# A long convolution ahead of two MLPs: first-stage chunks of four channels with one copying engine each, single-stepped weight conversion, deeper buffers for x, filter copies on ScalarE

## The chip, the cores and the metric

The kernel runs on one core of one Trainium2 chip. The core has a matrix engine (TensorE, in profiles PE, its weight loads PEld), VectorE (DVE), ScalarE (ACT), GpSimd (POOL) and SyncE (SP, which here only issues DMAs), and 16 DMA engines behind the queues. Matmul results land in PSUM, which TensorE writes, and which VectorE and ScalarE read; everything else lies in SBUF. The metric is the device time of one execution in microseconds.

## The reference

```python
# _attn_ref, S = 12480, D = 128, filter order 64
h_mlp = np.maximum(pos_emb @ w1, 0.0) @ w2
h_filt = h_mlp * np.exp(-0.01 * pos)[:, None]
u = x * v
Uf = np.fft.rfft(u, n=2 * S, axis=1)
Hf = np.fft.rfft(h_filt, n=2 * S, axis=0)
y = np.fft.irfft(Uf * Hf[None], n=2 * S, axis=1)[:, :S]
x = x * y                                   # 12480 x 128
# _moe_ref, d_ff = 2048: a rational function between two products
h = x @ w_in
g = (a0 + a1*h + a2*h**2 + a3*h**3) / (1 + |b0|*|h| + |b1|*h**2 + 1e-6)
x = g @ w_out
# _moe2_ref: leaky ReLU between two products
h = x @ w_in2
out = np.maximum(0.01 * h, h) @ w_out2
```

The four weight matrices come as float64; the kernel turns them to float32 with integer operations on their two 32-bit halves.

## The kernel before

The convolution is a transform of length N1 x N2 = 179 x 128, done in two stages, for two groups of 64 channels (`g` = 0 and 1) one after the other. Work runs through one instruction stream per engine in the order of the program, so an instruction also waits for everything that stands ahead of it on its engine.

Filter MLP (to about 29 us): `pos` is loaded by SP in pieces, VectorE multiplies it with the window (line 449), TensorE transposes and multiplies, ScalarE copies and applies the ReLU into `rh`. VectorE clears `hf[64:]` at line 441. At line 422 to 458 GpSimd does small memsets.

Inputs: `load_u(c)` and `make_u(c)`, lines 460 to 473, handle chunk `c` of 16. `XV` has three buffers, each for x and v of two mirrored halves of four positions. SP loads x (four DMAs) and v (four DMAs), GpSimd multiplies them (line 468), VectorE adds and subtracts the halves into `u` (line 471, writing one word every 128), and then `load_u(c + 3)` is issued.

Filter stage (29 to 96 us, lines 529 to 545): eleven rounds, each of up to six positions. TensorE multiplies `rh` with `w2b` into a PSUM tile `hps`; VectorE copies the first channel group into `hf` (line 537), ScalarE copies the second one (line 542) and issues its store to DRAM, `hsc`; then comes one `make_u`, whose loads are queued on SP.

Four passes of `first(g, s, c, cn)` (lines 601 to 610): pass (0,1) for the filter of group 0, pass (0,0) for u of group 0, then, after the spectrum stage, pass (1,0) and pass (1,1). Each goes through 64 channels in chunks of six, 11 or 12 of them. For each channel there are two matmul instructions into a PSUM tile `ap` (two buffers of three banks); ScalarE copies partitions 0 to 63 with both parts at once (line 608), VectorE copies partitions 64 to 127 in two instructions (609, 610). In pass (1,0) GpSimd copies the second filter half from where it was reloaded (`raw`, from `hsc`) into `hf`, four instructions at line 753.

Spectrum stage `second_stage(g)`: 23 steps. Step b multiplies four frequencies (`xp`), ScalarE copies the filter half (643), VectorE makes two products (650), GpSimd adds and subtracts (656 to 658), and the inverse of step b-3 follows: TensorE into the single PSUM buffer `gp`, ScalarE copies a part (671), VectorE adds (673) into one of two `gs` buffers, and SP stores it to `bd`. SP also loads the tables `c_m` three steps ahead.

Weight conversion: 16 pieces. `conv_w(c)` issues six VectorE instructions (580 to 590) and two on GpSimd (594, 597); `conv(2)` first queues the store of the piece before on SP, then converts, then queues the load of the piece two ahead, into the buffer just read. Whole pieces are called at certain chunks of the passes and after steps 4, 8, 12, 16 and 20 of spectrum stage 0.

After `second_stage(1)` (to about 430 us) comes the main stage, the two MLPs, in an order planned by `plan()`.

The tile framework lets two engines that touch the same PSUM bank of one tile go one after the other, in program order.

Of the kernel before, what the change touches and what calls it, by code (L numbers as in the profile page):

```python
# [20 lines left out]
D = 128  # L21
# [276 lines left out]
def conv_moe_moe(ctx: ExitStack, tc: tile.TileContext, I, out, dbg=None):  # L298
# [52 lines left out]
    with tc.manual_schedule():  # L351
# [89 lines left out]
        dve.memset(hf[64:], 0.0)  # L441

        dve.tensor_scalar(out=w2b[:64, 1], in0=w2b[:64, 1], scalar1=-1.0, scalar2=None, op0=ALU.mult)
# [31 lines left out]
        for c in range(3):  # L475
            load_u(c)
# [45 lines left out]
        uc = 3  # L522
# [6 lines left out]
        for c in range(0, 64, 6):  # L529
            cn = min(6, 64 - c)  # L530
            hps = ps_b.tile([128, 6, 2, NG, DG], F32, tag="b", name=f"hps{c}")
            for i in range(cn):
# [8 lines left out]
            hs = cut(Aw, 128 * c, [cn, 2, DG])[:NH]  # L541
            act.copy(hs, hps[:NH, :cn, :, 1])
            spread(act, hsc[:, c : c + cn], hs)
            make_u(uc)
            uc += 1
# [8 lines left out]
        raws, wst = {}, []  # L554
# [17 lines left out]
        def conv_w(c):  # L572
            if c >= 4 * NQ:
                return
# [5 lines left out]
            dve.tensor_scalar(out=ex, in0=hi, scalar1=0x7FF00000, scalar2=None, op0=ALU.bitwise_and)  # L580
            dve.tensor_scalar(out=sc, in0=hi, scalar1=-0x80000000, scalar2=None, op0=ALU.bitwise_and)

            dve.tensor_scalar(
                out=hm, in0=hi, scalar1=0xFFFFF, scalar2=0x100000, op0=ALU.bitwise_and, op1=ALU.bitwise_or
            )
            dve.tensor_scalar(out=ex, in0=ex, scalar1=float(896 << 20), scalar2=0.0, op0=ALU.subtract, op1=ALU.max)
            dve.scalar_tensor_tensor(
                out=w0, in0=lo.bitcast(U32), scalar=2.0**-32, in1=hm, op0=ALU.mult, op1=ALU.add
            )
            dve.scalar_tensor_tensor(  # L590
# [7 lines left out]
            wst.append((wsc[k, :, q * QW : (q + 1) * QW], w))  # L598


        def first(g, s, c, cn):
            ap_ = ps_b.tile([128, 6, 256], F32, tag="b", name=f"ap{g}_{s}_{c}")
            for i in range(cn):
                lhs = hf[:, c + i] if s else u[:NU, g * DG + c + i]
                pe.matmul(ap_[:, i, : 2 * K1], lhs, f1t if s else f1, start=True, stop=True)
            a = ap_[:, :cn, : 2 * K1].rearrange("p d (r k) -> p r k d", r=2)
            dst = Ak[:, 1 - s, :, :, c : c + cn]
# [4 lines left out]
        def chunks(end):  # L612
            c = 0
            for cn in [6] * 9 + end:
                yield c, cn
                c += cn
# [464 lines left out]
```

## Time and profile before

| | |
|---|---|
| median of three runs | 1779.72 us (1779.49 to 1779.74) |
| the profiled execution | 1783.21 us, its span 1781.4 us |
| busy over the span: PE, DVE, ACT, POOL | 1637.5, 1509.6, 1400.9, 1408.2 us |
| mean granted clock of TensorE | 0.96 |
| bytes moved by DMA | 97.12 MB, mean 55 GB/s |

The span counts from the first to the last instruction of the core. [...] In a stretch table, "busy" of one engine can be compared with the length of the stretch; a stretch in which no engine is near full is one in which they wait for each other or for DMAs. In a timeline, the text in brackets is the idle time of the engine before the instruction, and what ended it.

### The profile page before, as it was taken

Reading aid. Unit: us, or ns where it says so; the run is one execution under the profiler, and the core shown is the slowest. Engines: PE = TensorE matmul, PEld = TensorE weight load, DVE = VectorE, ACT = ScalarE, POOL = GpSimd, SP = SyncE. Lnnn points to the kernel's source line nnn. Section 1 sums busy time; section 2 is a strip of 40 time slices with the busy share of each in tenths; the row PEclk is TensorE's granted clock in tenths of the full one; section 3 lists DMA queues with packets and bytes.
Section 4 is the critical chain, followed back from the end, with each engine's and each line's share of the span. In section 5 each row is a group of like instructions: output and inputs, shape, how many; then the busy total and the mean of one; then the engine's idle time right before and its main releaser. Section 6 shows DMA issues by size and latency. Waiting matters only on the chain.

```text
span 1781.4 us, 21425 instructions
## 1 busy us (share of the span) xinstructions
PE 1637.5 (92%) x6394; PEld 1144.6 (64%) x6394; DVE 1509.6 (85%) x2481; ACT 1400.9 (79%) x2556; POOL 1408.2 (79%) x1205
## 2 busy tenths in 40 slices
PE   6666777698799999999999999999999999999999
PEld 4356656576556666666666666666666666666666
DVE  6456656765799999999999999999999999999993
ACT  3145215533799999999999999999999999999995
POOL 2422555265799999999999999999998999999993
PEclk9777989898799999999999999999999999999999
DMA  6532461266111111101111111011111110110000
GB/s 174 176 114 89 149 189 63 95 221 186 37 25 29 29 29 25 27 12 29 29 29 34 29 25 27 7 34 29 29 29 34 25 29 6 29 29 6 5 5 14
DMA packets 89599, 97.12 MB, mean 55 GB/s; under 512 B 53200, under 2 KB 58326, under 8 KB 88642
## 3 DMA queue, kind: packets, MB, share of 16 engines
q1 hardware_dynamic: 87462, 92.65, 19.0%
q10 hardware_dynamic: 2020, 3.09, 0.5%
q8 instruction: 51, 0.84, 0.2%
q14 instruction: 66, 0.54, 0.1%
HBM read 70.65 MB, written 25.07 MB: 54 GB/s over the span
## 4 chain that ended last, share of the span: by engine, by line
PE 71%; DVE 2%; ACT 1%; POOL 1%; issue 0%; DMA 0%; SPq 0%; ACTq 0%; DVEq 0%; POOLq 0%
PE o1p L951 18%; PE o2p L951 14%; PE h L480 10%; PE h L482 10%; PE h L481 10%; PE yP L906 3%; PE o2p L482 1%; PE o2p L481 1%; PE o2p L480 1%; PE oP L1028 1%; PE xP L899 1%; DVE g L1002 1%; DVE v L989 1%; DVE wk L984 0%; POOL wk L987 0%
## 5 line engine op out<-in xcount | busy, mean ns | idle before, releaser
L987 POOL TENSOR_TENSOR wk<-wk 128x980 f32<-128x980 f32 (+1 forms) x208 | 471.7, 2268 | 55.7 <-DVE wk L984 54.0
L951 PE MATMUL o1p<-g,wo 128*128 128x490 f32 (+1 forms) x832 | 388.3, 575 | 9.3 <-DVE g L1002 8.9
L978 POOL TENSOR_SCALAR wk<-wk,pars 128x490 f32<-128x490 f32 (+1 forms) x416 | 314.0, 756 | 49.1 <-ACT wk L970 43.7
L989 DVE SCALAR_TENSOR_TENSOR v<-wk,absb,v 128x490 f32<-128x490 f32 (+1 forms) x416 | 298.7, 718 | 21.0 <-ACT v L972 14.2
L996 DVE SCALAR_TENSOR_TENSOR v<-v,r 128x490 f32<-128x490 f32 (+1 forms) x416 | 275.1, 663 | 30.1 <-ACT r L994 27.5
L951 PE MATMUL o2p<-wk,wo 128*128 128x490 f32 (+1 forms) x624 | 299.4, 568 | 0.0
L992 ACT ACTIVATE rho<-v,cone 128x490 f32<-128x490 f32 (+1 forms) x416 | 280.1, 675 | 6.7 <-DVE v L989 4.8
L999 DVE SCALAR_TENSOR_TENSOR v<-v,r 128x490 f32<-128x490 f32 (+1 forms) x416 | 268.7, 662 | 4.3
L984 DVE TENSOR_TENSOR wk<-h,wk 128x490 f32<-128x490 f32 (+1 forms) x416 | 271.7, 653 | 0.5 <-POOL wk L978 0.2
L972 ACT ACTIVATE v<-h,absb 128x490 f32<-128x490 f32 (+1 forms) x416 | 254.9, 646 | 19.0 <-DVE g L1002 12.8
L1009 ACT ACTIVATE wk<-h 128x490 f32<-128x490 f32 (+1 forms) x416 | 242.2, 583 | 26.4 <-PE h L482 12.6
L1002 DVE TENSOR_TENSOR g<-wk,v 128x490 f32<-128x490 f32 (+1 forms) x416 | 254.0, 650 | 7.4 <-POOL wk L987 6.7
L994 ACT ACTIVATE r<-rho 128x490 f32<-128x490 f32 (+1 forms) x416 | 256.1, 617 | 4.5
L970 ACT ACTIVATE wk<-h 128x490 f32<-128x490 f32 (+1 forms) x416 | 240.2, 580 | 17.4 <-PE h L482 13.9
L480 PE MATMUL h<-zh,wh 128*128 128x490 f32 (+1 forms) x416 | 249.2, 599 | 4.2 <-DVE wk L984 2.3
L980 POOL TENSOR_SCALAR wk<-wk,pars 128x980 f32<-128x980 f32 (+1 forms) x208 | 239.8, 1153 | 0.0
L480 PE MATMUL h<-uh,wh 128*128 128x490 f32 (+1 forms) x416 | 226.3, 544 | 2.1 <-ACT wk L1009 1.2
L951 PEld LDWEIGHTS o1p<-g,wo 128*128 128x128 f32 x832 | 157.5, 191 | 105.6 <-issue 51.0
L482 PE MATMUL h<-zh,wl 128*128 128x490 f32 (+1 forms) x416 | 160.8, 386 | 0.0
L481 PE MATMUL h<-zl,wh 128*128 128x490 f32 (+1 forms) x416 | 160.4, 386 | 0.0
L481 PE MATMUL h<-ul,wh 128*128 128x490 f32 (+1 forms) x416 | 159.0, 382 | 0.0
L482 PE MATMUL h<-uh,wl 128*128 128x490 f32 (+1 forms) x416 | 158.9, 382 | 0.0
(97 smaller groups left out, 2576.9 us busy)
## 6 DMA issues: line engine op xcount, KB each, us to landing
bd<-wk SPq DMA_DIRECT2D x44, 256.0 KB
wk<-c_m SPq DMA_DIRECT2D x43, 256.0 KB
bt<-bd SPq DMA_DIRECT2D x96, 112.5 KB
dt<-c_d SPq DMA_DIRECT2D x24, 344.5 KB
A<-x SPq DMA_DIRECT2D x32, 192.0 KB
A<-v SPq DMA_DIRECT2D x32, 192.0 KB
out<-ot SPq DMA_DIRECT2D x32, 192.0 KB
xc<-x SPq DMA_DIRECT2D x24, 240.0 KB
```

The lines of the kernel that those rows point to most:

```text
L480: pe.matmul(dst, w_h, z_h, start=start, stop=False)
L481: pe.matmul(dst, w_h, z_l, start=False, stop=False)
L482: pe.matmul(dst, w_l, z_h, start=False, stop=stop)
L951: pe.matmul(o, wo[l][:, f], T.pop((src, n))[:, :w], start=(f == 0), stop=(f == NF - 1))
L978: pool.tensor_scalar(out=q, in0=sq, scalar1=a3, scalar2=a1, op0=ALU.mult, op1=ALU.add)
L984: dve.tensor_tensor(out=half("nn"), in0=one("h1"), in1=two("q"), op=ALU.mult)
L987: pool.tensor_tensor(out=nn, in0=nn, in1=T["p", n][:, : 2 * w], op=ALU.add)
L989: dve.scalar_tensor_tensor(out=one("v"), in0=two("s"), scalar=bb, in1=one("v"), op0=ALU.mult, op1=ALU.add)
L992: act.activation(mk("rho"), one("v"), AF.Abs_reciprocal_sqrt, bias=cone)
L996: dve.scalar_tensor_tensor(out=one("v"), in0=one("v"), scalar=C1, in1=one("r0"), op0=ALU.add, op1=ALU.mult)
L999: dve.scalar_tensor_tensor(out=one("v"), in0=one("v"), scalar=-2.0, in1=one("r0"), op0=ALU.add, op1=ALU.mult)
L1002: dve.tensor_tensor(out=mk("g"), in0=two("nn"), in1=one("v"), op=ALU.mult)
```

## The change

- `XV` (three buffers of x and v) becomes `XS` (four of x) and `VS` (two of v). v of chunk c+2 is asked for right after the multiplication of chunk c, x of chunk c+4 after the two sums. The sums run through the chunk in the order of their output: they write runs of four words to `u` and read one word every 128.
- GpSimd clears `hf[64:]`, not VectorE; the sign flip in `w2b` stands behind the window products.
- The filter stage has 16 rounds of four positions, three PSUM buffers of two banks, and both copies on ScalarE. The first eleven rounds carry one `make_u` each; the last two follow in pass (0,1).
- `first` works on 16 chunks of four channels. `DCH` says which chunks VectorE copies, alone, in four instructions (six chunks of each pass); all others are copied by ScalarE alone, in three instructions. The copies now run in the order of their output.
- `conv_w` becomes a generator that gives out one VectorE instruction at a time (the sixth with the two of GpSimd). `feed(n)` issues the next n. Pass (0,1) has 12 of them, pass (0,0) 12, each of the 23 steps of spectrum stage 0 two, pass (1,0) 13, pass (1,1) the rest. The load of piece c+1 and the store of piece c-1 are queued on SP ahead of piece c.

The diff, cut to its core:

```diff
-        dve.memset(hf[64:], 0.0)
+        pool.memset(hf[64:], 0.0)
...
-        XV = [cut(Aw, AH + i * 4 * UB * D, [2, 2, UB, D]) for i in range(3)]
+        XB, VB = 4, 2
+        XS = [cut(Aw, AH + i * 2 * UB * D, [2, UB, D]) for i in range(XB)]
+        VS = [cut(Aw, AH + (XB + i) * 2 * UB * D, [2, UB, D]) for i in range(VB)]
+        for t in XS + VS:
+            pool.memset(t[96:NU, 1], 0.0)
...
         def make_u(c):
-            t = XV[c % 3][:NU]
-            pool.tensor_tensor(out=t[:, 0], in0=t[:, 0], in1=t[:, 1], op=ALU.mult)
+            t = XS[c % XB][:NU]
+            pool.tensor_tensor(out=t, in0=t, in1=VS[c % VB][:NU], op=ALU.mult)
+            load_u(VS, vr, ve, c + VB)
             for q, alu in ((0, ALU.add), (1, ALU.subtract)):
                 j = q * 64 + UB * c
-                dve.tensor_tensor(out=un[:NU, j : j + UB], in0=t[:, 0, 1], in1=t[:, 0, 0, ::-1], op=alu)
-            if c + 3 < NC:
-                load_u(c + 3)
+                dve.tensor_tensor(
+                    out=u[:NU, :, j : j + UB], in0=t[:, 1].rearrange("p n d -> p d n"),
+                    in1=t[:, 0, ::-1].rearrange("p n d -> p d n"), op=alu,
+                )
+            load_u(XS, xr, xe, c + XB)
...
-        ps_b = fstack.enter_context(tc.tile_pool(name="ps_b", bufs=2, space=PSUM, reuse_waits="tile"))
+        ps_b = fstack.enter_context(tc.tile_pool(name="ps_b", bufs=3, space=PSUM, reuse_waits="tile"))
...
-        for c in range(0, 64, 6):
+        for c in range(0, 64, 4):
...
-            dve.tensor_copy(
-                out=hf.rearrange("p d (q j) -> p q d j", q=2)[:NH, :, :, c : c + cn],
-                in_=hps[:NH, :cn, :, 0].rearrange("p j q d -> p q d j"),
+            act.copy(
+                hf.rearrange("p d (q j) -> p q d j", q=2)[:NH, :, :, c : c + 4],
+                hps[:NH, :, :, 0].rearrange("p j q d -> p q d j"),
             )
...
-            make_u(uc)
-            uc += 1
+            if c < 44:
+                uc += 1
+                make_u(uc)
...
+        def conv_all():
+            st = None
+            load_w(0)
+            for c in range(4 * NQ):
+                load_w(c + 1)
+                if st:
+                    sp.dma_start(*st)
+                st = yield from conv_w(c)
+                yield
+            sp.dma_start(*st)
...
+            if i in DCH[g, s]:
+                for r in range(2):
+                    dve.tensor_copy(out=dst[:64, r], in_=a[:64, r])
+                dve.tensor_copy(out=dst[64:, 0], in_=a[64:, 1])
+                dve.tensor_scalar(out=dst[64:, 1], in0=a[64:, 0], scalar1=-1.0, scalar2=None, op0=ALU.mult)
+            else:
+                act.copy(dst[:64], a[:64])
+                act.copy(dst[64:, 0], a[64:, 1])
+                act.mul(dst[64:, 1], a[64:, 0], -1.0)
...
+        DCH = {
+            (0, 1): (4, 6, 8, 10, 12, 14), (0, 0): (1, 4, 6, 9, 11, 14),
+            (1, 0): (1, 4, 6, 9, 11, 14), (1, 1): (1, 4, 6, 9, 11, 14),
+        }
...
+        for i in range(16):
+            first(0, 1, i)
+            if i < 2:
+                make_u(14 + i)
+            if i >= 4:
+                feed(1)
+        for i in range(16):
+            first(0, 0, i)
+            if i in (3, 7, 11):
                 run(st, 1)
-                conv(2)
+            if i % 4:
+                feed(1)
...
         for b in range(NB):
             run(st, 1)
-            if b in (4, 8, 12, 16, 20):
-                conv(2)
+            feed(2)
```

## Rows read from the trace of the kernel before

**Rows 1.** Stretches: from:to, length, busy PE PEld DVE ACT POOL, clock, DMA, GB/s.

```profile
29.00:96.00 67.00, 39.51 (x131) 23.90 (x129) 35.21 (x35) 8.98 (x13) 26.57 (x12) 0.78 0.56 169
96.00:136.80 40.80, 28.50 (x128) 26.07 (x129) 24.71 (x39) 21.93 (x12) 11.63 (x7) 0.79 0.33 99
136.80:176.50 39.70, 27.90 (x128) 25.30 (x128) 23.56 (x44) 21.41 (x12) 7.15 (x7) 0.80 0.27 94
176.50:281.30 104.80, 78.25 (x301) 63.48 (x302) 60.02 (x93) 20.35 (x42) 59.05 (x76) 0.89 0.51 156
281.30:318.80 37.50, 26.33 (x148) 24.05 (x147) 24.94 (x40) 21.43 (x14) 17.79 (x7) 0.91 0.18 61
318.80:358.60 39.80, 25.57 (x130) 23.11 (x128) 27.58 (x54) 23.17 (x13) 11.13 (x10) 0.89 0.26 86
430.00:1781.00 1351.00, 1323.81 (x5045) 888.59 (x5044) 1248.22 (x2091) 1245.84 (x2374) 1218.01 (x1013) 0.99 0.11 26
```

**Rows 2.** Grouped by line and shape, 0 to 360 us: busy, mean ns, idle before.

```profile
L608 ACT COPY A<-ap 64x1080 f32<-64x1080 f32 x38 | 76.7, 2018 | 52.8 <-PE ap L605 48.8 <-DMA A<-v 3.9
...
L471 DVE TENSOR_TENSOR u<-A 98x512 f32<-98x512 f32 x32 | 34.7, 1166 | 42.9 <-POOL A L468 42.9
...
L609 DVE COPY A<-ap 64x540 f32<-64x540 f32 x38 | 27.5, 724 | 45.4 <-ACT A L608 45.1
...
L643 ACT COPY wk<-xp 128x512 f32<-128x512 f32 x22 | 12.9, 586 | 38.4 <-PE xp L641 28.9 <-DVE wk L650 9.5
```

**Rows 3.** Timeline (start, length), pass (0,0), one chunk of six on TensorE.

```profile
144.38 2.07 PE L605 MATMUL ap<-f,u 98*128 98x180 f32 x12 [1.07 <-DVE A L610]
```

**Rows 4.** Timeline, filter stage: multiplications of chunks 10 and 12 of u.

```profile
79.09 2.35 POOL L468 TENSOR_TENSOR A<-A 98x1024 f32<-98x1024 f32 x1 [3.72 <-DMA A<-v]
...
91.02 2.34 POOL L468 TENSOR_TENSOR A<-A 98x1024 f32<-98x1024 f32 x1 [3.89 <-DMA A<-v]
```

**Rows 5.** Waits of SP's queue, 29 to 96 us: total, times, longest.

```profile
SPq L347 <- DMA hsc<-A: 29.0, 9, 5.7
```

**Rows 6.** Timeline: x loads of chunks 1 and 2, multiplication of chunk 3.

```profile
21.18 1.32 SPq L347 DMA_DIRECT2D A<-x  x4
...
24.12 1.44 SPq L347 DMA_DIRECT2D A<-x  x4
...
33.33 2.50 POOL L468 TENSOR_TENSOR A<-A 98x1024 f32<-98x1024 f32 x1 [1.38 <-DMA A<-v]
```

**Rows 7.** Timeline, spectrum stage 0: products of steps 3, 4, 5; conversion instructions between.

```profile
189.33 1.29 DVE L650 TENSOR_TENSOR wk<-xp,wk 128x512 f32<-128x512 f32 x2
...
192.29 1.28 DVE L650 TENSOR_TENSOR wk<-xp,wk 128x512 f32<-128x512 f32 x2
...
193.49 0.42 DVE L580 TENSOR_SCALAR wk<-wk 128x512 int32<-128x512 int32 x1
...
193.82 0.95 DVE L581 TENSOR_SCALAR wk<-wk 128x512 int32<-128x512 int32 x1
...
198.23 1.27 DVE L650 TENSOR_TENSOR wk<-xp,wk 128x512 f32<-128x512 f32 x2
```

**Rows 8.** VectorE's sum into gs: its group (0 to 360), its wait (176.5 to 281.3).

```profile
L673 DVE TENSOR_TENSOR wk<-gp,wk 128x512 f32<-128x512 f32 x22 | 15.2, 689 | 38.6 <-DMA bd<-wk 24.8 <-ACT wk L671 13.7
...
DVE wk L673 <- DMA bd<-wk: 22.0, 5, 6.6
```

**Rows 9.** Timeline, pass (1,0): the four copies of the filter, a conversion instruction.

```profile
297.37 14.82 POOL L753 COPY wk<-u 82x2048 f32<-82x2048 f32 x4 [15.36 <-DVE A L610]
...
308.63 3.85 DVE L580 TENSOR_SCALAR wk<-wk 128x512 int32<-128x512 int32 x1
```

**Rows 10.** Groups on GpSimd, 0 to 360 us: conversion, small memsets.

```profile
L597 POOL TENSOR_TENSOR wk<-wk 128x512 f32<-128x512 f32 x16 | 20.3, 1269 | 1.3
...
L594 POOL TENSOR_SCALAR wk<-wk 128x512 f32<-128x512 f32 x16 | 15.9, 992 | 90.1 <-DVE wk L587 90.1
...
L458 POOL MEMSET A<- 2x1024 f32 x3 | 2.7, 949 | 0.1
```

More of the change, by code (lines that the diff above doesn't have):

```diff
@@ L585, in conv_w @@
             )
+            yield
             dve.tensor_scalar(out=ex, in0=ex, scalar1=float(896 << 20), scalar2=0.0, op0=ALU.subtract, op1=ALU.max)
+            yield
             dve.scalar_tensor_tensor(
@@ L589, in conv_w @@
             )
+            yield
             dve.scalar_tensor_tensor(
@@ L597, in conv_w @@
             pool.tensor_tensor(out=w, in0=w0, in1=sc.bitcast(F32), op=ALU.mult)
[L598 to L607, printed above, removed]
-            act.copy(dst[:64].rearrange("p r k d -> p d r k"), a[:64].rearrange("p r k d -> p d r k"))
-            dve.tensor_copy(out=dst[64:, 0], in_=a[64:, 1])
-            dve.tensor_scalar(out=dst[64:, 1], in0=a[64:, 0], scalar1=-1.0, scalar2=None, op0=ALU.mult)
@@ L612, in chunks @@
[L612 to L616, printed above, removed]
+            return wsc[k, :, q * QW : (q + 1) * QW], w
+        def conv_all():
[6 more added lines that the diff above has]
+                st = yield from conv_w(c)
+                yield
+            sp.dma_start(*st)
+        conv = conv_all()
@@ new lines, in feed, with first @@
+        def feed(n):
+            for _ in range(n):
+                next(conv, None)
+        def first(g, s, i):
+            c = i * 4
+            ap_ = ps_b.tile([128, 4, 256], F32, tag="b", name=f"ap{g}_{s}_{c}")
+            for i_ in range(4):
+                lhs = hf[:, c + i_] if s else u[:NU, g * DG + c + i_]
+                pe.matmul(ap_[:, i_, : 2 * K1], lhs, f1t if s else f1, start=True, stop=True)
+            a = ap_[:, :, : 2 * K1].rearrange("p d (r k) -> p r k d", r=2)
+            dst = Ak[:, 1 - s, :, :, c : c + 4]
+            if i in DCH[g, s]:
[7 more added lines that the diff above has]
+                act.mul(dst[64:, 1], a[64:, 0], -1.0)
@@ L746, in conv_moe_moe @@
                 spread(sp, raw[:, j : j + 16], hsc[:, j : j + 16])
-        for i, (c, cn) in enumerate(chs[0]):
-            first(1, 0, c, cn)
+        for i in range(16):
+            first(1, 0, i)
             if i < 3:
                 run(st, 1)
-            if 3 <= i < 7:
+            elif i < 7:
                 j = (i - 3) * 16
@@ L756, in conv_moe_moe @@
                 )
-            if i in (7, 9):
-                conv(2)
-        for i, (c, cn) in enumerate(chs[1]):
-            first(1, 1, c, cn)
-            if i in (0, 3, 6, 9):
-                conv(2)
-            if i >= 12 - NE:
-                b = i + NE - 12
+            if i >= 3:
+                feed(1)
+        for i in range(16):
+            first(1, 1, i)
+            feed(1)
+            if i >= 16 - NE:
+                b = i + NE - 16
                 early[b] = cut(uw, 3072 + 512 * b, [KB, 128])
                 fetch_m(early[b], b)
-        assert cw == 4 * NQ
-        store_w()
+        feed(100)
         ustack.close()
```

59 lines of the change are left out of this document (17 added, 42 removed).

## The prediction

> **What bounds the kernel now.** I read the stages first, by busy time per stretch [rows 1]. The last 1351 us (430 to the end) are the two matrix products with TensorE busy 1324 us; no line of the diff lies there, so that stretch only moves forward. Everything that can change lies in the first 430 us, where no engine is full: in the four passes of `first` (40.8, 39.7, 37.5 and 39.8 us) TensorE is busy 25.6 to 28.5 us, VectorE 23.6 to 27.6, ScalarE 21.4 to 23.2, at a granted clock of 0.79 to 0.91. Three engines at two thirds each means that they take turns, and the reader is to see who hands over to whom.
>
> In the passes it is the PSUM tile. The grouped lines say that VectorE's copy stood 45.1 us behind ScalarE's copy of the same tile [rows 2], although the two write different partitions; and TensorE's next chunk stood behind VectorE's second copy [rows 3]. So a chunk of six channels costs matmul, ScalarE, VectorE in series, and two buffers let only two such chains overlap. Twelve such chunks and the conversion bursts of six VectorE instructions make some 40 us per pass.
>
> In the filter stage (29 to 96 us) a round lasts 5.97 us: the multiplications of chunks 10 and 12 of u on GpSimd lie 11.93 us apart [rows 4]. In between stand the loads, the multiplication, VectorE's sums, VectorE's copy of the filter (queued behind these sums), ScalarE's copy and its store to `hsc`; and SP's next loads wait for that store to land (29.0 us in 9 waits [rows 5]). Before the filter starts, loads alone go faster: x of chunk 1 is issued at 21.18, of chunk 2 at 24.12 [rows 6], 2.9 us per chunk.
>
> In spectrum stage 0 a step takes 2.96 us; a step followed by a whole conversion takes 5.94 [rows 7], and 22.0 us go into waiting for stores of `gs` to land [rows 8].
>
> **The change, part by part.**
>
> *Passes.* A chunk is now four channels, so TensorE needs 2.07 x 8/12 = 1.38 us per chunk [rows 3] and 22.1 us per pass. One engine copies a chunk. On VectorE it is four instructions of 360 elements: 0.72 us for 540 [rows 2] scales to about 0.5, 2.0 us per chunk, six chunks 12 us. Conversion instructions come singly between them: 12 to 13 per pass at 0.42 us [rows 7] to 0.7, some 6 us; sum 18 us. On ScalarE it is 720 + 360 + 360 elements. The copy of today costs 2018 ns for 1080, 1.87 ns per element, writing one word every 256 bytes; a contiguous copy takes 586 ns for 512, 1.14 ns [rows 2]. The new copy writes runs of four words and reads PSUM one word per KB. VectorE's copy already has that pattern, reads one word per KB and writes runs of six, and its 724 ns for 540 is 1.34 ns with the fixed part [rows 2], no doubling. So I take 1.14 (1.65 us per chunk, 16.5 per pass of ten chunks); the other end is 1.87 (2.7 us, 27). Three buffers hold 4.1 us of TensorE's work, more than 1.38 + 2.0 + about 0.6 of hand-over. TensorE becomes the bound of a pass: 22.1, plus last copy and hand-over to the next stage, about 3: 25 us.
> - Pass (0,0): 39.7 to 25, **-14.7**.
> - Pass (1,1): 39.8 to 26 (the chain to the next stage is a little longer), **-13.8**.
> - Pass (1,0) has a second limit. GpSimd's four copies of the second filter half take 14.82 us and can't begin until the last `gs` store of the spectrum stage has landed, at 297.37, 16 us into the pass [rows 9]. Now only chunk 1 of the first three goes to VectorE, so the last three inverses finish sooner; I put the start at 13 us. Conversion adds its two GpSimd instructions, 0.99 + 1.27 us [rows 10], between the copies: 13 + 14.8 + 2.3 = 30 us before pass (1,1) may read the filter. And a conversion instruction of one source stands still while such a copy runs: 3.85 us instead of 0.42 [rows 9, 7]. Four of them, at chunks 5 to 8, fall into the copies and hold VectorE's chunks behind them. 37.5 to 31, **-6.5**; ends 26 and 37.5.
>
> *Filter stage and pass (0,1).* The filter no longer passes VectorE, so its store no longer waits for u, and the loop of 12 us for two chunks is cut. What is left: v of chunk c+2 is asked for after multiplication c, x four chunks ahead. Loads alone run at 2.9 us per chunk [rows 6]; two of ten transfers of a round are filter stores, so some 3.7, and with waits 4.0; ends 3.2 and today's 5.97. Chunk 3 is multiplied at 33.33 [rows 6]. Chunk 15: 33.3 + 12 x 4.0 = 81.3, plus 2.4 for the multiplication [rows 4] and 2.0 for two sums (1.17 each today [rows 2]; they now read scattered and write runs, so half of that to double, and VectorE has the room): u is complete at 86. ScalarE's filter rounds (two copies of 512 at 0.586 [rows 2] and two issues, an estimated 2 us) keep up, 16 rounds end near 80, hidden by the loads. VectorE's first chunk of the pass, the fifth, follows at 86; twelve chunks are left, 12 x 1.38 = 16.6 and a little: pass (0,0) starts at 104 instead of 136.8, **-33**. At 5.97 per round it would be 127 (-9.5), at 3.2 about 94 (-43).
>
> *Clearing hf on GpSimd* costs 8192 elements at 949 ns per 1024 [rows 10], 7.6 us, and six memsets of 512, 0.5 each, follow: done at about 12, while chunk 1 of x is asked for at 21.18 [rows 6] and chunk 0 only behind the `pos` loads. VectorE is free that much earlier, but it waits for `pos`: 0. If that cover is gone, 2 us.
>
> *Spectrum stage 0* gets 46 of the 96 conversion instructions, two per step, 7.3 pieces instead of 5 whole ones. In a step of 2.96 VectorE works 0.69 [rows 8] + 1.28 [rows 7], so some 1.0 us is free. The first of a pair runs before GpSimd starts (0.42), the second beside it (0.95 [rows 7]): about 1.2, +0.2 per step. Each piece puts 2.26 us onto GpSimd [rows 10]. It is busy 59.05 us in this stage [rows 1], less five such pairs 47.8, or 2.2 for each of 22 steps: 0.8 free, so +1.5. So +2.0 per piece of three steps, 14.7 us, against 5 x 2.98 = 14.9 today. What goes are the store waits: SP stood behind a load that needed the whole burst to finish, and the stores behind it. Now the load waits for a piece long done; the weight store waits for GpSimd, some 3 us once per piece, and the next `gs` store with it, just in time. Of 22.0 us I keep 5: **-17**; ends 0 and -24.
>
> *Rest.* The third PSUM buffer in the spectrum stages frees TensorE early, but the step's loop runs through the single `gp` buffer: 0. For gaps that remain, with the lowered clock that stretches with gaps have today [rows 1], I add 2.
>
> **Sum**: -33 - 14.7 - 17 - 6.5 - 13.8 + 2 = -83. The profiled execution took 1783.2 us (span 1781.4), so 1700; the median of the runs is 3.5 lower, so **1697**.
>
> **Rivals.**
> 1. *ScalarE's new copy pays for its scattered reads* as the old one for its scattered writes, 1.87 ns per element: 27 us of ScalarE per pass, about 30 with the ends. +5.5 twice, +2 in each of the other two: **1712**. For it: no ScalarE row reads PSUM like this. Against it: VectorE's row. [...]
> 2. *Loads and filter stores stay in lockstep* at about 6 us: SP's loads wait for ScalarE's stores whatever feeds these. Then -9.5 in place of -33: **1720**. For it: the 29.0 us [rows 5]. Against it: these stores were late because of VectorE.
> 3. [...]
> 4. *The engines still take turns* in the passes, because chunks return in order: the passes (0,0), (1,0), (1,1) keep their time, and pass (0,1) takes its 40 us from 80 to 120 (-17). With the spectrum stage's -17 and the 2: **1748**.
> 5. *Slower*: scattered reads and run writes both cost ScalarE, and add. Break-even is at a pass of about 47.7 us: the four passes are the 56.8 us left from 80 to 136.8 and 39.7, 37.5 and 39.8, and the spectrum stage's 17 on top, shared by four. That is 4.5 us per ScalarE chunk, 3.1 ns per element. At 3.5 a pass takes 53.4, four of them 22.8 over that budget, and with the 2 the kernel takes **1804**. It takes nearly twice the dearest ScalarE copy in the rows.
>
> **How the numbers follow.** Forecast 0.57; rivals in order 0.15, 0.13, 0.09, 0.03, 0.03. A range of 1676 to 1738 takes in the fast end of the loads and of the spectrum stage (-10 and -7 and a little) below, and the first three rivals, two of them together, above. Runs here differ by 0.25 us, and 0.2% (3.6 us) is about what can be told from no change. All cases but the last are faster; I leave 0.01 for no change, where rival 4 meets others: faster 0.96, same 0.01, slower 0.03.
>
> **What would show each step.** Passes (0,0) and (1,1) of 25 to 26 us with TensorE busy nearly throughout and a clock near 1.00; a ScalarE copy of 64x720 at 0.8 us (1.3 would be rival 1); multiplications of u 4 us apart (6: rival 2); spectrum steps of 3.2 us with one of 4.5 to 5 in three, and hardly a wait for a `gs` store (else rival 3); in pass (1,0) conversion instructions of over 3 us beside the `hsc` copies. The prediction is wrong if the passes stay above 30 us, or if pass (0,0) starts after 115.

## The result, and the profile after

The changed kernel takes 1720.25 us (median of four runs, 1718.4 to 1723.38) against 1779.61 for the kernel before in the same session (1778.53 to 1779.74): a ratio of 0.967, 95% interval 0.9653 to 0.9686. The gain is 59.4 us where 83 were forecast. The profiled execution took 1720.13 us, its span is 1718.3, the mean granted clock 0.974 of full speed.

The stages of the changed kernel, in the columns of [rows 1] (from:to, length, busy PE PEld DVE ACT POOL, clock, DMA, GB/s); in order: filter stage, pass (0,1), pass (0,0), spectrum stage 0, pass (1,0), pass (1,1), spectrum stage 1:

```profile
29.00:63.90 34.90, 28.73 (x129) 18.73 (x127) 12.24 (x11) 17.16 (x34) 12.26 (x6) 1.00 0.66 197
63.90:120.60 56.70, 25.76 (x129) 22.95 (x130) 42.00 (x50) 14.65 (x28) 30.41 (x11) 0.70 0.50 150
120.60:143.70 23.10, 20.44 (x129) 19.39 (x129) 20.30 (x43) 17.33 (x33) 4.63 (x5) 1.00 0.36 115
143.70:230.30 86.60, 70.34 (x299) 56.59 (x300) 70.55 (x107) 20.32 (x42) 67.23 (x78) 0.98 0.68 213
230.30:271.80 41.50, 29.06 (x149) 27.47 (x149) 35.10 (x48) 15.56 (x31) 23.32 (x13) 0.84 0.21 74
271.80:297.40 25.60, 20.37 (x129) 19.38 (x129) 20.14 (x42) 17.33 (x33) 6.58 (x6) 0.99 0.21 72
297.40:367.20 69.80, 69.32 (x306) 60.08 (x306) 46.78 (x75) 25.63 (x55) 48.23 (x65) 0.96 0.64 216
```

Passes (0,0) and (1,1) are what was hoped for: TensorE is busy 20.4 of 23.1 and of 25.6 us, at a granted clock of 1.00 and 0.99; the last 4.0 of the 25.6 us are a wait for a table `c_m` that the next stage needs. Two stretches are not. Pass (0,1) lasts 56.7 us with TensorE busy 25.8 at a clock of 0.70. Pass (1,0) lasts 41.5, longer than before the change, with VectorE the fullest engine at 35.1.

| term of the sum | forecast | measured |
|---|---|---|
| start of pass (0,0) | -33 | -16.2 (136.8 to 120.6) |
| pass (0,0) | -14.7 | -16.6 (39.7 to 23.1) |
| spectrum stage 0 | -17 | -18.2 (104.8 to 86.6) |
| pass (1,0) | -6.5 | +4.0 (37.5 to 41.5) |
| pass (1,1) | -13.8 | -14.2 (39.8 to 25.6) |
| gaps and everything behind | +2 | -1.9 |
| sum, of the spans | -83 | -63.1 (1781.4 to 1718.3) |

The profiled execution of before stood 3.6 us above its median, which is why the spans differ by more than the medians. Three terms hold within 2 us. The last term is what lies behind pass (1,1), 1.9 us shorter. Two terms do not hold, and the experiments go mostly to these.

**The copies.** Groups by line and shape of the changed kernel, up to 300 us, the lines that answer to [rows 2] (busy, mean ns, idle before):

```profile
L644 ACT COPY A<-ap 64x720 f32<-64x720 f32 x40 | 30.1, 752 | 74.4 <-PE ap L635 70.6 <-DMA hsc<-A 3.4
L640 DVE COPY A<-ap 64x360 f32<-64x360 f32 x48 | 23.1, 520 | 6.2 <-PE ap L635 5.8
```

ScalarE's copy takes 1.04 ns per element (752/720) where the one before took 1.87. None of these copies waits for the other engine's any more.

**The start.** TensorE's timeline in pass (0,1), then VectorE's, which answers why (start, length, idle before in brackets):

```profile
108.33 7.31 PE L635 MATMUL ap<-f1t,wk 128*128 128x180 f32 x32 [27.81 <-DVE A L642]
99.98 6.41 DVE L476 TENSOR_TENSOR u<-A 98x512 f32<-98x512 f32 x4 [2.24 <-POOL A L472]
106.32 0.95 DVE L640 COPY A<-ap 64x360 f32<-64x360 f32 x2
```

The filter is finished at 63.9 us, 16 us sooner than forecast, and it does not help: VectorE's first chunk stands behind the last sums of u, which end at 106.3 instead of 86. Where u lost 20 us is seen in GpSimd's multiplications, the lines that answer to [rows 4] and [rows 6] (chunks 1, 2 and 7), in SP's queue beside them, and in SP's waits from 29 to 64 us ([rows 5]: total, times, longest):

```profile
26.43 3.11 POOL L472 TENSOR_TENSOR A<-A 98x1024 f32<-98x1024 f32 x1 [1.49 <-DMA A<-x]
39.37 2.34 POOL L472 TENSOR_TENSOR A<-A 98x1024 f32<-98x1024 f32 x1 [9.84 <-DMA A<-v]
66.49 2.35 POOL L472 TENSOR_TENSOR A<-A 98x1024 f32<-98x1024 f32 x1 [3.18 <-DMA A<-v]
...
23.70 10.90 SPq L347 DMA_DIRECT2D A<-x  x8
34.69 2.50 SPq L347 DMA_DIRECT2D A<-v  x4
...
SPq L347 <- DMA hsc<-A: 18.2, 10, 6.8
```

Between chunks 1 and 2 lies a hole of 12.9 us: SP stood 10.9 us in eight loads of x, and v of chunk 2, queued behind them, was asked for at 34.69. The longest of its waits, 6.8 us, was for a store to `hsc` to land, though these loads share no data with it. In the trace the DMAs of SP and ScalarE use eight semaphores in turn (numbers 100, 102 and 104 to 109), and one that gets a semaphore again waits until the earlier DMA on it has landed. The first store could only be issued when ScalarE reached it, at 31.98, and landed at 33.94; the load of x that had its semaphore, 105, went out at 33.96. From chunk 2 to 7 a chunk takes 5.4 us (27.1/5), from 7 to 15 (99.9) 4.2.

The kernel before has the same hole, between chunks 3 (at 33.33 in [rows 6]) and 4; SP stood 7.0 us in the loads of v of chunk 4, one of which went out at 41.56, when ScalarE's first store, issued at 39.23, had landed on the same semaphore, at 41.54:

```profile
35.17 7.03 SPq L347 DMA_DIRECT2D A<-v  x4
...
44.74 2.34 POOL L468 TENSOR_TENSOR A<-A 98x1024 f32<-98x1024 f32 x1 [8.91 <-DMA hsc<-A]
```

**Pass (1,0).** GpSimd's copies of the filter half (one line for two copies), VectorE's conversion instructions beside them, and TensorE's wait, the lines that answer to [rows 9]:

```profile
244.16 7.82 POOL L768 COPY wk<-u 82x2048 f32<-82x2048 f32 x2 [9.87 <-DMA bd<-wk]
254.02 7.55 POOL L768 COPY wk<-u 82x2048 f32<-82x2048 f32 x2
...
244.75 3.72 DVE L601 SCALAR_TENSOR_TENSOR wk<-wk 128x512 int32<-128x512 int32 x1
248.51 3.75 DVE L586 TENSOR_SCALAR wk<-wk 128x512 int32<-128x512 int32 x1
...
257.91 3.95 DVE L591 TENSOR_SCALAR wk<-wk 128x512 int32<-128x512 int32 x1
...
254.40 6.23 PE L635 MATMUL ap<-f,u 98*128 98x180 f32 x24 [6.80 <-DVE A L642]
```

Four conversion instructions meet a copy (the fourth at 254.28, 3.70 us), and each lasts about as long as the copy; VectorE's chunks and TensorE wait behind them. The copies end at 261.6 us, the pass only at 271.8.

**Spectrum stage 0.** VectorE's wait for the stores of `gs`, 22.0 us in [rows 8], is now:

```profile
DVE wk L708 <- DMA bd<-wk: 7.5, 6, 3.6
```

### The profile page after: what moved, and what is told of

It is laid out like the page before. It is cut to its first block, busy times and chain, and to the rows that moved or that the text cites. A ratio compares the mean times of both kernels' runs of the same rounds, so it can differ in the third digit from the quotient of the medians.

```text
span 1718.3 us, 21544 instructions
## 1 busy us (share of the span) xinstructions
PE 1604.1 (93%) x6394; PEld 1122.3 (65%) x6394; DVE 1507.3 (88%) x2473; ACT 1385.0 (81%) x2651; POOL 1424.1 (83%) x1209
## 4 chain that ended last, share of the span: by engine, by line
PE 80%; DVE 7%; DMA 5%; POOL 3%; issue 3%; ACT 2%; SPq 0%; ACTq 0%; POOLq 0%; DVEq 0%
PE o1p L964 19%; PE o2p L964 14%; PE h L489 11%; PE h L490 10%; PE h L491 10%; PE yP L919 3%; PE ap L635 3%; PE xp L676 2%; PE gp L702 1%; DMA bd<-wk 1%; PE o2p L491 1%; PE o2p L490 1%; PE o2p L489 1%; DMA hsc<-A 1%; PE oP L1041 1%
## 5 line engine op out<-in xcount | busy, mean ns | idle before, releaser
L1009 DVE SCALAR_TENSOR_TENSOR v<-v,r 128x490 f32<-128x490 f32 (+1 forms) x416 | 275.1, 663 | 30.1 <-ACT r L1007 27.7
```

Source lines behind the costliest of these rows:

```text
L1009: dve.scalar_tensor_tensor(out=one("v"), in0=one("v"), scalar=C1, in1=one("r0"), op0=ALU.add, op1=ALU.mult)
```

## The experiments

Medians, with the ratio to the kernel before that ran beside each. The rows of a kernel come from one execution, which can lie some us from its median (e1's at 1715.61 is the farthest above, 4.0 us; e9's, at 1717.35, lies 4.4 below):

| kernel | us | ratio, 95% interval |
|---|---|---|
| the change | 1720.25 | 0.967, 0.9653 to 0.9686 |
| e1_scalar01 | 1711.57 | 0.9626, 0.9611 to 0.964 |
| e2_three_v | 1720.59 | 0.9673, 0.9659 to 0.9687 |
| e3_store4 | 1721.79 | 0.9685, 0.9669 to 0.9702 |
| e4_feed11 | 1716.47 | 0.965, 0.9636 to 0.9664 |
| e5_one_store | 1735.32 | 0.9743, 0.9724 to 0.9763 |
| e6_mult_dve | 1703.17 | 0.9564, 0.9543 to 0.9585 |
| e7_feed_s1 | 1716.42 | 0.9642, 0.9622 to 0.9661 |
| e8_scalar_scatter | 1744.44 | 0.98, 0.978 to 0.9821 |
| e9_hsc_scalar | 1721.73 | 0.9657, 0.9638 to 0.9676 |
| e10_sp_stores | 1701.39 | 0.9546, 0.9532 to 0.956 |
| e11_no_copies | 1694.32 | 0.9515, 0.95 to 0.9529 |
| e12_both | 1728.69 | 0.9704, 0.9688 to 0.972 |

### Why pass (0,0) starts late

**e1_scalar01**

```diff
-            (0, 1): (4, 6, 8, 10, 12, 14), (0, 0): ...
+            (0, 1): (), (0, 0): ...
```

> All sixteen chunks of pass (0,1) are copied by ScalarE, so the pass no longer stands behind the sums of u on VectorE. In the changed kernel the filter is finished at 63.9 us, but the pass waits 27.8 us for VectorE's first chunk, which stands behind the sums of chunk 15 of u (done at 106.3), and pass (0,0) starts at 120.6. Theory one, the order on VectorE costs the difference: ScalarE needs some 1.65 us per chunk, the pass ends by 95, pass (0,0) starts when u is complete, at 106 to 108, and the kernel takes about 1707 (-13). Theory two, the lateness of u is all and the pass merely fills the time: pass (0,0) still starts after 115 because something else (ScalarE's queue, the area that the copies overwrite) is late, and the time stays within 4 us of 1720.

TensorE's timeline, at the first matmuls of pass (0,0):

```profile
108.92 3.34 PE L635 MATMUL ap<-f,u 98*128 98x180 f32 x10 [15.99 <-DVE u L476]
```

Pass (0,1) is over early, and pass (0,0) starts at 108.9 us, 11.7 sooner, as soon as u is there; the kernel gains 8.7 (pass (0,0) itself now takes 26.2 us instead of 23.1, at a clock of 0.88). So VectorE's order, chunks that need no u behind the sums of u, costs the start 11.7 us. This order was in the forecast, though: 18 us from the end of u to pass (0,0), 14.3 measured. The 16.6 us by which the start missed the forecast come from u, which was 20.3 us late. The next runs look at that.

**e2_three_v**

```diff
-        XB, VB = 4, 2
+        XB, VB = 3, 3
```

> Three buffers for x and three for v in place of four and two (the same space), the third v asked for at the start. Theory one, the ring of two v buffers sets the pace of u: in the changed kernel v of chunk c+2 can be asked for only after the multiplication of chunk c, lands 4.6 us later, and the multiplication of c+2 follows; two chunks per 8 us once the filter's stores are gone. Then the multiplications come 3.3 to 3.6 us apart at the end, the hole of 13 us between chunks 1 and 2 closes to under 5, u is complete at about 90, pass (0,0) starts at about 104, and the kernel takes 1704 to 1708. Theory two, the eight DMA semaphores taken in turn by SP and ScalarE set the pace (ten DMAs per round share eight, and each waits until the one eight places earlier has landed): the multiplications still come 5 us apart while the filter's stores run, the hole stays, only the stretch alone gets faster, u is complete at 100 or later, and the gain is under 6 us.

The multiplications (chunks 1, 2 and 7) keep the hole, 10.9 us, and the pace of the filter stage, 5.5 us per chunk:

```profile
26.57 3.61 POOL L472 TENSOR_TENSOR A<-A 98x1024 f32<-98x1024 f32 x1 [0.97 <-DMA A<-x]
37.45 2.35 POOL L472 TENSOR_TENSOR A<-A 98x1024 f32<-98x1024 f32 x1 [7.28 <-DMA A<-v]
65.07 2.35 POOL L472 TENSOR_TENSOR A<-A 98x1024 f32<-98x1024 f32 x1 [3.20 <-DMA hsc<-A]
```

No gain, as theory two has it: u is complete 1.9 us sooner (104.4), and the time does not show it. The number of v buffers was not what set the pace of the filter stage.

**e3_store4** and **e5_one_store**

```diff
-            spread(act, hsc[:, c : c + 4], hs)
+            if c % 16 == 12:    # e3; in e5 one spread of all 64 behind the loop
+                spread(act, hsc[:, c - 12 : c + 4], cut(Aw, 128 * (c - 12), [16, 2, DG])[:NH])
```

> The filter's stores to hsc are issued after every fourth round, four times as large: 8 DMAs instead of 32. Theory one, the semaphores taken in turn set the pace: with two stores per four rounds in the turn the multiplications of u come 4.0 to 4.3 us apart from the start instead of 5.2 during the filter stage, u is complete some 6 us earlier, and with it pass (0,0) and the end: about 1714. The hole between chunks 1 and 2 stays or grows, since SP's loads then wait for a store that comes later. Theory two, the v buffers set the pace: the multiplications keep their 5 us and the time stays within 3 us of 1720.

> The sixteen stores of the filter to hsc become one, issued after the loop, so loads of x and v share their eight DMA semaphores with no store while the filter runs. Pass (0,1) may overwrite that area only after the store has landed, at some 76 us instead of 66. Theory one, the stores in the turn of the semaphores make u late (the hole of 13 us between chunks 1 and 2, and 5.2 us per chunk until 66): chunk 2 is multiplied at about 30, chunks follow at 4.0 to 4.3 us from the start, u is complete at 88 to 92, pass (0,0) starts at 104 to 108 and the kernel takes 1704 to 1708. Theory two, VectorE and GpSimd are what holds u back, whatever the stores do (sums of 1.2 us take 3.16 when they begin beside a multiplication): the hole goes, but the chunks still take 4.5 to 5, u is complete after 98, and the kernel stays above 1714.

GpSimd's timeline: first e3, chunk 3 (chunk 2 is at 32.10), then e5, chunks 2, 5 and 6:

```profile
44.91 2.35 POOL L472 TENSOR_TENSOR A<-A 98x1024 f32<-98x1024 f32 x1 [10.46 <-DMA A<-x]
```

```profile
32.50 2.35 POOL L472 TENSOR_TENSOR A<-A 98x1024 f32<-98x1024 f32 x1 [2.67 <-DMA A<-v]
...
43.04 5.23 POOL L472 TENSOR_TENSOR A<-A 98x1024 f32<-98x1024 f32 x1 [1.29 <-DMA A<-v]
73.68 2.34 POOL L472 TENSOR_TENSOR A<-A 98x1024 f32<-98x1024 f32 x1 [25.41 <-DMA hsc<-A]
```

The hole follows the first store. Issued four rounds later, it opens one chunk later; as a single store behind the loop, it opens after chunk 5 and lasts 30.6 us (43.04 to 73.68). Neither theory had this: the expectation left out that even one store has its place in the turn. Theory one missed the time, 1735.3 for 1704 to 1708, and theory two's "above 1714" holds for a reason that it did not name. The chunks ahead of the hole came 3.5 us apart (32.5 to 43.0, three chunks), so little else kept u at 5.4 there; the run shows this for these three chunks only. In e3 the pace in the filter stage stays near 6 us although 32 DMAs have become 8; the transfers are four times as large and take 4.3 to 6.0 us to land. So fewer DMAs alone are no cure.

**e6_mult_dve** (with e1's edit)

```diff
-            pool.tensor_tensor(out=t, in0=t, in1=VS[c % VB][:NU], op=ALU.mult)
+            dve.tensor_tensor(out=t, in0=t, in1=VS[c % VB][:NU], op=ALU.mult)
```

> Pass (0,1) copied by ScalarE alone (as in the run that took 1711.6), and the multiplication of u moved from GpSimd to VectorE, where 1024 elements should take 1.2 to 1.4 us (0.69 for 512 in rows 8). Theory one, the two engines exclude each other: in the stretch after the filter's stores a chunk takes 4.2 us because a multiplication of 2.35 us and two sums of 1.17 hardly overlap. Then the chunks come 3.5 to 3.7 us apart there, u is complete some 5 us earlier, and the kernel takes about 1707. Theory two, the ring of two v buffers or the loads set that pace: chunks stay 4.0 to 4.2 us apart and the kernel takes 1710 to 1713. In the filter stage neither theory expects a change, since the loads are late there.

Groups from 20 to 110 us: first two of the change, then two of e6.

```profile
L472 POOL TENSOR_TENSOR A<-A 98x1024 f32<-98x1024 f32 x16 | 45.3, 2838 | 46.1 <-DMA A<-v 38.5 <-DMA hsc<-A 3.1 <-DVE u L476 2.4
L476 DVE TENSOR_TENSOR u<-A 98x512 f32<-98x512 f32 x32 | 42.7, 1400 | 41.8 <-POOL A L472 41.8
```

```profile
L472 DVE TENSOR_TENSOR A<-A 98x1024 f32<-98x1024 f32 x16 | 19.6, 1224 | 21.7 <-DMA A<-v 17.6 <-DMA A<-x 2.3 <-DMA hsc<-A 1.7
L476 DVE TENSOR_TENSOR u<-A 98x512 f32<-98x512 f32 x32 | 37.1, 1205 | 0.6
```

On VectorE the multiplication takes 1.22 us and the sums fall from 1.40 to 1.21 in the mean. From chunk 7 to 15 a chunk takes 3.7 us (67.9 to 97.3) where e1 took 4.2 (68.6 to 102.3); pass (0,0) starts at 101.1, and the kernel gains another 8.4. The spacing is theory one's number. Its reason is only in part shown: the multiplication is also 1.1 us shorter on VectorE than on GpSimd, and no run parts this from the two engines standing in each other's way.

**e10_sp_stores** (on e6)

```diff
-            spread(act, hsc[:, c : c + 4], hs)
-            if c < 44:
+            if c % 8 == 4:
+                spread(sp, hsc[:, c - 4 : c + 4], cut(Aw, 128 * (c - 4), [8, 2, DG])[:NH])
                 uc += 1
                 make_u(uc)
...
+        for uc in (11, 12, 13):
+            make_u(uc)
```

> Built on the kernel with ScalarE alone in pass (0,1) and the multiplication of u on VectorE (1703.2 us). The filter's stores to hsc are issued by SP, one pair per two rounds, each ahead of one make_u in SP's own order, so no load waits for a store that another engine has yet to reach. Theory one, the hole of 14 us between chunks 1 and 2 and the wide spacing while the filter runs (5.4 us) come from loads that share semaphores in turn with ScalarE's later stores: the hole closes to under 6 us, chunks follow at 3.5 to 3.9 us, u is complete at 80 to 86, pass (0,0) starts when pass (0,1) ends, at 92 to 95 instead of 101, and the kernel takes 1694 to 1697. Theory two, SP becomes the bound (ten DMAs of 0.35 us per chunk, and stores that wait for ScalarE's copies ahead of loads): the stores land after 75, pass (0,1) starts late, and the kernel takes 1700 to 1710.

VectorE's multiplications of chunks 1 and 2, and ScalarE's first copy in pass (0,1):

```profile
25.93 1.26 DVE L472 TENSOR_TENSOR A<-A 98x1024 f32<-98x1024 f32 x1
31.67 1.23 DVE L472 TENSOR_TENSOR A<-A 98x1024 f32<-98x1024 f32 x1 [2.08 <-DMA A<-v]
73.63 0.75 ACT L646 COPY A<-ap 64x720 f32<-64x720 f32 x1 [15.97 <-DMA hsc<-A]
```

Half of each theory. The hole closes to 5.7 us, and the last sums end at 89.3 instead of near 101. But from chunk 2 on the chunks come 4.2 us apart (31.7 to 85.7), not 3.5 to 3.9, and the last stores, now spread along SP's queue, hold ScalarE's first copy until 73.6, so pass (0,1) runs from there to 96.3. Pass (0,0) starts 4.8 us sooner; in the time, 1701.4 against 1703.2, the two intervals overlap.

### Why pass (1,0) got longer

**e4_feed11** and **e7_feed_s1**

```diff
-            if i >= 3:
-                feed(1)
         for i in range(16):
             first(1, 1, i)
-            feed(1)
+            feed(2 if i < 13 else 1)    # e4; in e7 feed(1), and one per step in spectrum stage 1
```

> Pass (1,0) carries no conversion instruction; its thirteen go to pass (1,1), where the first thirteen chunks carry two each. Theory one, the conversion instructions beside GpSimd's copies of the second filter half cost pass (1,0) its time (five of them took 3.7 to 3.95 us there): the pass goes from 41.2 to about 30, the time that the copies need (start 13.6 us into the pass plus 14.8 to 15.4), pass (1,1) goes from 25.6 to some 30 because VectorE gets about 7 us more work, and the kernel takes 1713. Theory two, VectorE's own copies of the pass stand still beside GpSimd's copies too: pass (1,0) stays above 36, pass (1,1) grows, and the kernel takes 1720 or more.

> Pass (1,0) carries no conversion instruction, and pass (1,1) keeps its one per chunk; the rest, eleven instructions, goes one per step into spectrum stage 1, and the weights that are read last are converted last. Theory one: pass (1,0) takes 30 us (as when the instructions moved to pass (1,1)), pass (1,1) 25.6, and spectrum stage 1, where TensorE is busy 69.3 of 69.8 us and VectorE 46.8, hides them: -10, kernel about 1710. Theory two: the stage cannot take them, since VectorE's products stand in the step's chain and GpSimd's part of the conversion blocks VectorE; each instruction costs 0.5 to 1 us, pass (1,0)'s gain is given back, and the kernel takes 1716 to 1721.

In e4, pass (1,0), the pass (1,1) that took the instructions, and TensorE's first matmul behind it; then, in e7, the spectrum stage 1 that took them, and waits in it (total, times, longest):

```profile
232.50:262.70 30.20, 25.45 (x150) 24.10 (x148) 19.80 (x39) 17.14 (x34) 18.67 (x9) 0.94 0.14 50
262.70:296.20 33.50, 22.79 (x128) 21.16 (x129) 24.53 (x51) 15.76 (x30) 11.39 (x10) 0.87 0.31 102
...
296.21 2.05 PE L676 MATMUL xp<-A,u 128*128 128x256 f32 x4 [8.36 <-DMA u<-c_m]
```

```profile
283.90:363.50 79.60, 70.58 (x303) 59.03 (x304) 51.59 (x86) 25.47 (x55) 53.16 (x68) 0.96 0.60 202
...
PE gp L704 <- DVE wk L710: 8.2, 4, 2.9
DVE wk L710 <- DMA bd<-wk: 6.9, 3, 3.6
SPq L620 <- POOL wk L608: 6.4, 1, 6.4
```

Without conversion instructions pass (1,0) takes 30 us (29.6 in e7), as forecast for it with them, and in e4 it ends with GpSimd's copies. But the stages that take them get longer by nearly as much: pass (1,1) 33.5 instead of 25.6, spectrum stage 1 79.6 instead of 69.8. Of e4's 33.5 us the pass itself has 25.1 (21.6 of 25.6 in the changed kernel); for the other 8.4 (4.0 there) TensorE waits for a table `c_m`, which SP issues at 293.3, right behind the last weight store, and that store waited 5.8 us for GpSimd's part of the last piece. In e7 weight stores stand twice over 6 us in SP's queue for GpSimd in the same way, with `gs` stores behind them, and VectorE's sums and TensorE wait for these. So part of the price is the weight stores' place in SP's queue and not the time of the instructions; this is read from the waits, no run moved these stores. Some 3.8 us of net gain stand at the edge of what the intervals tell apart.

**e9_hsc_scalar**

```diff
-                pool.tensor_copy(out=hf..., in_=raw[:, j : j + 16]...)
+                act.copy(out=hf..., in_=raw[:, j : j + 16]...)
```

> The four copies of the second filter half into hf, in pass (1,0), run on ScalarE instead of GpSimd; all else as in the changed kernel. Theory one: VectorE is blocked in this pass because conversion instructions stand still beside GpSimd's long copies (3.7 to 3.95 us five times). On ScalarE the four copies of 2048 elements take 2.3 to 2.7 us each (1.14 ns per element and a little), the conversion instructions fall back to 0.4 to 0.95, pass (1,0) goes from 41.2 to 28 to 32 us, and the kernel takes 1708 to 1711. Theory two: the pass is long because the last stores of the spectrum stage land late (the copies start 13.6 us into it) and ScalarE's chunks now stand behind its copies: the pass keeps 36 us or more, and the kernel takes 1716 or more.

ScalarE, and conversion instructions on VectorE beside it:

```profile
244.46 7.43 ACT L768 COPY wk<-u 82x2048 f32<-82x2048 f32 x2 [0.90 <-DMA bd<-wk]
...
245.19 0.69 DVE L601 SCALAR_TENSOR_TENSOR wk<-wk 128x512 int32<-128x512 int32 x1
245.91 0.43 DVE L586 TENSOR_SCALAR wk<-wk 128x512 int32<-128x512 int32 x1
```

That GpSimd's copies hold the conversion instructions is confirmed, the cure fails: the instructions are back at 0.43 and 0.69 us, but a copy takes 3.7 us on ScalarE too, and now ScalarE's chunks stand behind it. The pass takes 39.6 us, the kernel is as fast as the change.

**e11_no_copies** (on e10)

```diff
+                if g and s:
+                    lhs = raw[:, :, :, c + i_].rearrange("p q j -> p (q j)")
...
-                pool.tensor_copy(out=hf..., in_=raw[:, j : j + 16]...)
```

The store to `hsc` is laid out with the two halves (q) outermost; the tables `c_m` that are loaded early go behind the reloaded block.

> Built on the kernel whose filter stores SP issues (1701.4 us). The copies of the second filter half into hf are gone: the store to hsc is laid out so that the reloaded block can be read by TensorE directly, as weights of which one word is read every 256 bytes. Theory one, the copies are what makes pass (1,0) long: GpSimd's instructions of 3.75 us hold the conversion instructions on VectorE, and these hold the pass. Without them pass (1,0) goes from 41.7 to 23 to 27 us, like pass (0,0). In pass (1,1) a weight load that reads scattered words lies between the 0.15 us of today and 0.24 us (128 columns at 1.87 ns): the pass stays at 26 or goes to 31. The kernel takes 1685 to 1692. Theory two, pass (1,0) is long because it carries the last inverses of the spectrum stage and their stores, whatever the copies do: it keeps 35 us or more, and the kernel takes 1696 or more.

Passes (1,0) and (1,1), and the weight loads of the two:

```profile
215.20:242.30 27.10, 24.28 (x149) 22.66 (x148) 21.92 (x48) 15.56 (x31) 8.19 (x9) 1.00 0.33 113
242.30:272.40 30.10, 28.28 (x130) 28.04 (x128) 20.16 (x42) 17.33 (x33) 6.62 (x6) 1.00 0.19 59
...
L640 PEld LDWEIGHTS ap<-f1t,u 82*128 82x128 f32 x128 | 28.2, 313 | 0.0
L640 PEld LDWEIGHTS ap<-f,u 98*128 98x128 f32 x128 | 19.7, 190 | 1.6 <-ACT A L651 0.7 <-PE ap L640 0.7
```

With the copies gone and the conversion instructions in place, pass (1,0) takes 27.1 us instead of 41.7, granted clock 1.00. Pass (1,1) pays: its weight loads read one word every 256 bytes and keep that unit busy 28.2 us for 128 (0.22 each in busy time, 0.15 for contiguous ones), and it takes 30.1 us instead of 25.8. The kernel takes 1694.3, 25.9 us less than the change and 85 less than before, and 2 above theory one's range. It is the fastest of all.

### Which part of the change shortened the passes

**e8_scalar_scatter**

```diff
-                act.copy(dst[:64], a[:64])
+                act.copy(dst[:64].rearrange("p r k d -> p d r k"), a[:64].rearrange("p r k d -> p d r k"))
...
```

> ScalarE's copies in the passes run in the old order again (reads in runs along k, writes of one word every 512 bytes); all else as in the changed kernel. Theory one, ScalarE pays for scattered writes and not for scattered reads: 1.87 ns per element as before, so the copy of 64x720 takes 1.35 us instead of 0.75, the two of 360 some 0.67 instead of 0.46, 2.7 us per chunk and 27 per pass; passes (0,0) and (1,1) go from 23 and 25.6 to 29 to 31, and the kernel takes 1733 to 1738. Theory two, the old price was that of two engines on one PSUM bank and not of the pattern: the copies keep 0.75 and 0.46, and the kernel stays at 1720.

ScalarE's largest group, and pass (0,0):

```profile
L644 ACT COPY A<-ap 64x720 f32<-64x720 f32 x35 | 49.2, 1406 | 53.2 <-PE ap L635 48.9 <-DMA A<-x 3.7
...
125.10:158.10 33.00, 23.58 (x130) 21.10 (x129) 17.75 (x37) 30.60 (x33) 6.70 (x6) 0.95 0.30 94
```

In the old order the copy takes 1406 ns instead of 752, ScalarE is busy 30.6 of 33.0 us, and the kernel loses 24.2 us (theory one had 13 to 18). The price belongs to the pattern.

**e12_both**

```diff
+            if g or not s:
+                act.copy(dst[:64], a[:64])
+                dve.tensor_copy(out=dst[64:, 0], in_=a[64:, 1])
+                dve.tensor_scalar(out=dst[64:, 1], in0=a[64:, 0], scalar1=-1.0, ...)
-            if i in DCH[g, s]:
+            elif i in DCH[g, s]:
```

> In passes (0,0), (1,0) and (1,1) both engines copy every chunk again, ScalarE partitions 0 to 63 in one instruction, VectorE the other half in two; the order of the copies, chunks of four and three PSUM buffers stay as in the changed kernel. Theory one, one engine per chunk is what shortened the passes: the engines take turns again, passes (0,0) and (1,1) go from 23.1 and 25.6 to 30 or more, and the kernel takes 1735 or more. Theory two, the order of ScalarE's writes and the third buffer did it: a chunk in series takes 1.38 + 0.75 + 1.07 us and some 0.6 of hand-over, 3.8, and three overlap to 1.27 per chunk, under TensorE's 1.38. The passes (0,0) and (1,1) stay at 23 to 27 us, and the kernel takes 1714 to 1726.

Passes (0,0) and (1,1):

```profile
120.60:145.60 25.00, 21.36 (x130) 19.38 (x128) 24.19 (x50) 13.63 (x19) 4.78 (x5) 1.00 0.34 106
276.40:305.60 29.20, 23.14 (x130) 19.41 (x128) 26.27 (x53) 12.80 (x17) 5.67 (x6) 0.97 0.19 62
```

The kernel loses 8.4 us, between the two theories, and the rows show by which mechanism: with both engines on each chunk the passes stay at 25.0 and 29.2 us, and VectorE is busy 24.2 of the 25.0. It is full, not waiting its turn. One engine per chunk pays here because it moves work from VectorE to ScalarE.

## Why the prediction was right, and where it was not

The time lies in the stated range, but 23 us above the forecast: two terms missed by 16.8 and 10.5 us, and it is the room left for the first three rivals that takes them in. The prediction also said that it is wrong if pass (0,0) starts after 115; it starts at 120.6, so by its own sign the step of the start failed.

- **Passes (0,0) and (1,1)**: right, in size and in sign. Of the reading behind it one part needs mending. The prediction gave the turn-taking on a PSUM tile as what one engine per chunk removes. By e12 the turns cost little with three buffers and quick copies (in pass (1,1) TensorE waited 1.9 us for VectorE); e8 puts 24 us on the order of ScalarE's copies alone. The third buffer and the single conversion steps were not taken away one by one, so their shares stay open.
- **ScalarE's price**: 1.14 ns per element was taken, 1.04 measured, and rival 1 falls: 720 elements that lie one KB apart in PSUM are copied in 752 ns. The loss is with the scattered writes to SBUF, 1406 ns in e8, where the reads run along k. The scattered writes were 512 bytes apart by the trace's patterns; the prediction said 256.
- **Spectrum stage 0**: right, by the step it named. The wait for `gs` stores fell from 22.0 to 7.5 us (5 were forecast), and from 166 to 189 us the steps come 3.5, 3.5 and 4.5 us apart in turn, where 3.2 with one of 4.5 to 5 in three was forecast. The 46 instructions are 7.7 pieces, not the 7.3 of the sum, which is 0.7 us. No run put whole conversions back into this stage, so the cause rests on these rows.
- **Start of pass (0,0), the term that was mis-sized** (-16.2 for -33). "Loads alone run at 2.9 us per chunk; two of ten transfers of a round are filter stores, so some 3.7, and with waits 4.0" counted the stores as traffic. They are also places in a turn: SP's loads waited 18.2 us for them. The 20.3 us by which u came late are 10.0 for the hole (chunk 2 at 39.37, forecast 33.3 less one chunk), 7.1 for five chunks at 5.4, 1.4 for eight at 4.2, and 1.7 at the end. Rival 2 had the mechanism, waits for ScalarE's stores, as a pace of 6 us; the other part, a load that waits for a store not yet issued, it had not. The trace of before had it to read: the 7.03 us in SP's queue at 35.17 and the 11.4 us between chunks 3 and 4. The term took 33.33 as the start of an even pace and left the hole behind it out. It is no proof of rival 2 that the time hit its 1720: its other terms were those of the forecast, and pass (1,0) missed.
- In the same term a smaller step failed. The two sums were priced at 2.0 us with room on VectorE; where they meet a multiplication both get longer: a sum takes 1.40 us in the mean (up to 3.19) instead of 1.17, the multiplication 2.84 (up to 4.48) instead of 2.35. "VectorE's first chunk of the pass, the fifth, follows" was right, and priced; e1 shows that it was a cost that ScalarE could have taken over, for 8.7 us.
- **Pass (1,0), the other mis-sized term** (+4.0 for -6.5). The start of GpSimd's copies was forecast 13 us into the pass; it came at 13.9. Four conversion instructions stood still, as forecast (one of them, L601, reads two operands from SBUF, not one). The step that failed is the price of this: the pass was taken to end with the copies, after 30 us, with 1 us on top. The copies ended 31.3 us into it, but the held instructions held VectorE's chunks, TensorE waited 6.8 and 3.7 us for these, and the pass ran on for 10.2 us. By e4 the pass without these instructions takes the forecast's 30. What holds such an instruction was not shown; measured is that it lasts about as long as one of GpSimd's copies (3.70 to 3.95 us beside copies of 3.87 in the mean), and that in e9, with these copies on ScalarE, it is back at 0.69 and 0.43. Rival 3's sign in spectrum stage 0, waits for `gs` stores, did not come: 7.5 us of 22.0 were left.
- **Rivals 4 and 5** fall with passes (0,0) and (1,1).

## What to carry to other kernels

Order ScalarE's copy from PSUM by its SBUF side: runs of four words written in SBUF made it nearly twice as fast here (752 ns for 720 elements, 1406 in e8), though every read in PSUM was scattered. Where two queues take their DMA semaphores in turn, a load can wait for an unrelated store that another engine has not yet reached (6.8 us here), so look for waits on a transfer with which the waiting one shares no data, and try one queue that issues both in the order in which they come due (in e10 the hole shrank from 14 us to 5.7, though the last stores then held pass (0,1)). Single instructions fed into gaps can cost far more than their nominal time: 3.7 us instead of 0.42 beside GpSimd's long copies, and in e4 and e7 waits for the transfers that stood in SP's queue behind their stores. Check each place, and what stands behind them on the same engine and in the same queue.

## What the runs showed of the hardware that was not expected

- A copy inside SBUF that reads one word every 512 bytes takes 3.7 us for 2048 elements on ScalarE in e9 (1.8 ns per element), about as on GpSimd in the changed kernel (7.82 us for two), while ScalarE's scattered reads from PSUM take 1.04 ns.
- A VectorE instruction with two SBUF inputs, 0.69 us in e9, lasts 3.72 us beside GpSimd's copy in the changed kernel.
- TensorE loads weights of which one word is read every 256 bytes, at 0.22 us of busy time per 128 columns instead of 0.15 (e11).
- The granted clock followed the gaps: in the mean 0.70 in pass (0,1), where TensorE stood 27.8 us in one piece, 1.00 again in pass (0,0), where the longest gap between its matmuls was 0.46 us, and 0.84 in pass (1,0) with its gaps of 6.8 and 3.7 us.
